# Turned queries and key-value products in two single-bank tiles, batch 0 between the weight blocks, one value scaling and one Pool chunk per tile

## The chip, the cores and the metric

One core of a Trainium2 chip runs the kernel. The metric is the device time of one execution in microseconds (us). Times are medians of the runs given; a profile is one execution with the hardware profiler. A run more than 1.5% above the fastest of the same kernel is called slow; ratios use the other, fast runs alone. PE is the tensor engine, PEld its weight loads, DVE the vector engine, ACT the scalar engine, POOL (Pool) the GpSimd engine. A "tile" below is one of 36 groups of 128 tokens; tile n's *attend* is the group of products that starts its work, and I use the start of attend as the time mark of the tile. The *clock* is the share of full speed that PE was granted. PSUM is the memory into which PE writes its products, in banks; SBUF is the memory of all other tiles. The *fold* is the product of the two weight matrices, and the *bias add* (DVE) is the last computation on a tile. A *ring* of two is a pair of buffers used in turn.

## The reference, cut to what matters

Eight batches, eight heads, 576 positions, head size 64. Linear attention with cosine and sine weights, then a two-layer network with softplus:

```python
r = np.maximum(x, 0.0);  phi = np.concatenate([r * c, r * s], axis=-1)   # for q and k
kv  = np.einsum('bhsf,bhsd->bhfd', k_p, v);   z = np.sum(k_p, axis=2)
num = np.einsum('bhsf,bhfd->bhsd', q_p, kv)
den = np.einsum('bhsf,bhf->bhs', q_p, z)[..., None] + 1e-06
x   = (num / den).transpose(0, 2, 1, 3).reshape(B * S, H * D)            # 4608 x 512
h = x @ w_in;  g = np.maximum(h, 0.0) + np.log1p(np.exp(-np.abs(h)));  out = g @ w_out
```

The kernel replaces softplus by LN2 + h/2, so that both weights fold into one matrix W_c = w_in w_out / 2 and a bias. Squares of x and of the weights check afterwards that the inputs allow it; a full path stands behind an `If`.

## The kernel before: the parts that matter here

Two PSUM tiles of two banks (`big_ps`) serve attend, the key-value products and the fold; two one-bank tiles (`qt_ps`) serve the turned queries. The queries of a batch are turned (transposed and multiplied by cosine and sine) one batch ahead.

```python
def relu_q(b, hq, engine):
    if hq == 0:
        q_rs[b] = work.tile([128, 2, T, 2, D], BF16, tag="q_r", name="q_r")   # ring of two
    engine.tensor_scalar(q_rs[b][:, hq], ..., BIG, 0.0, ALU.min, ALU.max)

def scale_values(b, hq, c):      # DVE, two SBUF inputs, cosine (c=0) or sine half (c=1)
    nc.vector.tensor_mul(view(vcs, ...), kqv[b, "v"][:, 2*hq : 2*hq+2], view(cs_wide, ...))

def relu(b):                     # Pool: one gate, then three rectifications in a row
    nc.gpsimd.tensor_copy(gate, vcs_bufs[(b - 1) % 2][:, 3, T - 1, 1, VW - 2 :])
    for hq in range(2):
        relu_q(b, hq, nc.gpsimd)
    relu_k(b, nc.gpsimd)
...                              # start: batch 0 whole, then weights, 16 squares, fold
for j, i in enumerate(mine):     # the loop over the tiles of batch b
    attend(i)
    for hq, c in itertools.islice(scales, 2 if j == 0 else 1):
        scale_values(b + 1, hq, c)
    if j == 2 and b + 2 < B:
        relu(b + 2)
    if more and j >= last - 1:
        key_values(b + 1, j - last + 1)
    some(1); turn_x(i - 1); some(1 if j < last else 9); emit(i - 2)   # cut: their conditions
```

The gate is a copy of two elements. It reads what the last scaling wrote, so Pool cannot begin to rectify before DVE has finished that scaling. The *row of eights* is the ninth block of 64 positions of each batch; those of an even and an odd batch share one tile (8, 17, 26, 35).

Of the kernel before, what the change touches and what calls it, by code (L numbers as in the profile page):

```python
# [21 lines left out]
def kernel(  # L22
# [31 lines left out]
    qt_ps = ctx.enter_context(tc.tile_pool(name="qt_ps", bufs=2, space=PSUM))  # L54
# [4 lines left out]
    def view(ap, *dims, offset=0):  # L59
        return bass.AP(  # L60
            tensor=ap.tensor, offset=ap.offset + offset,
            ap=[list(ap.ap[0])] + [list(d) for d in dims],
        )

# [12 lines left out]
    warm = singles.tile([128, 512], BF16)  # L77
    nc.vector.memset(warm, 1.0)
    load(0, "q", 0)
    load(0, "q", 1)  # L80


    idx_i = singles.tile([128, T], mybir.dt.int32)
# [4 lines left out]
    for part in range(2):  # L88
        load(0, "k", part)
        load(0, "v", part)  # L90

    xT_all = singles.tile([128, N_TOK // 128, KO, 128], BF16)
    w_in_sb = xT_all[:, 4 : 4 + D_FF // 128].rearrange("p n g t -> p (n g t)").rearrange(
        "p (ko f) -> p ko f", ko=KO
    )
    w_out_sb = singles.tile([128, FO, D_MODEL], BF16)
    for ko in range(KO):
        nc.gpsimd.dma_start(w_in_sb[:, ko, :], moe_w_in[ko * 128 : (ko + 1) * 128, :])
    w_out_r = moe_w_out.rearrange("(fo p) m -> p fo m", p=128)
    for f in range(0, FO, 4):  # L100
        nc.gpsimd.dma_start(w_out_sb[:, f : f + 4, :], w_out_r[:, f : f + 4, :])
    for b in (1, 2, 3):
        for name in ("q", "k", "v"):
            load(b, name)

    ones = singles.tile([128, 128], F32)
    nc.vector.memset(ones, 1.0)
    blk_bufs = []
    for r in range(3):
        blk = singles.tile([128, 2, 2, 2, C], BF16, name=f"kvblk{r}")  # L110
        nc.vector.memset(blk, 0.0)
        blk_bufs.append(blk)
# [11 lines left out]
    nc.scalar.copy(cs_wide, view(cs_col, [1, 2 * T], [0, D]))  # L124
    diag = singles.tile([128, T, 2, 128], BF16)
    for t in range(T):
        for c in range(2):
            nc.vector.tensor_scalar_mul(diag[:, t, c, :], ident, cs_col[:, c, t : t + 1])
    perm = singles.tile([128, 128], BF16)
    nc.vector.tensor_copy(view(perm, [2, 64], [1, 2]), view(ident, [1, 64], [64, 2]))  # L130
# [5 lines left out]
    def turn_w_in(ko, half):  # L136
        n = (2 * ko + half) % 3
        pool, tag = (xt_ps, "xt") if n == 0 else (qt_ps, "qt")
        ps = pool.tile([128, 8, 128], BF16, tag=tag, name="wT_ps")
        for j in range(8):  # L140
            ft = 8 * half + j
            nc.tensor.matmul(
                ps[:, j, :], w_in_sb[:, ko, ft * 128 : (ft + 1) * 128], ident,
                is_transpose=True, start=True, stop=True, skip_group_check=True,
            )
        dst = view(
            w_inT, [D_MODEL, 8], [128, 2], [1, 64],
            offset=8 * half * D_MODEL + 256 * (ko // 2) + 64 * (ko % 2),
        )
        src = ps.rearrange("p f (h d) -> p f h d", h=2)  # L150
        if half:
            nc.scalar.copy(dst, src)  # L152
        else:
            nc.vector.tensor_copy(dst, src)

    def fold(pair, quarter, ps):
        for ft in range(4 * quarter, 4 * quarter + 4):
            for j in range(2):
                g = 2 * pair + j
                nc.tensor.matmul(  # L160
                    ps[:, j, :], w_inT[:, ft, g * 128 : (g + 1) * 128], w_out_sb[:, ft, :],
                    start=(ft == 0), stop=(ft == FO - 1),
                )
# [32 lines left out]


    VW = D + 2
    vcs_bufs = []
    for r in range(2):  # L200
        vcs = singles.tile([128, 4, T, 2, VW], BF16, name=f"vcs{r}")
        vcs_bufs.append(vcs)

    def mark_values(r):
        for hp in range(4):
            at = 0 if hp % 2 else D
            nc.vector.tensor_copy(
                vcs_bufs[r][:, hp, :, :, at : at + 2], view(cs_col, [1, T], [T, 2], [0, 2])
            )

    def scale_values(b, hq, c):
        vcs = vcs_bufs[b % 2]
        nc.vector.tensor_mul(  # L213
            view(vcs, [T * 2 * VW + 2, 2], [2 * VW, T], [1, D],
                 offset=2 * hq * T * 2 * VW + c * VW),
            kqv[b, "v"][:, 2 * hq : 2 * hq + 2],
            view(cs_wide, [0, 2], [D, T], [1, D], offset=c * T * D),
        )

    def key_values(b, hq):  # L220
        vcs, blk, k_r = vcs_bufs[b % 2], blk_bufs[b % 3], kqv[b, "k"]
        kv = big_ps.tile([128, 2, 512], F32, tag="big", name="kv_ps")
        for t in range(T):
            for h2 in range(2):
                for i in range(2):
                    rows = slice(64 * h2, 64 * h2 + 64)
                    nc.tensor.matmul(  # L227
                        kv[64 * i : 64 * i + 64, h2, : 2 * VW],
# [3 lines left out]
        for i in range(2):  # L232
            rows, cols = slice(64 * i, 64 * i + 64), slice(65 * i, 65 * i + 65)
            nc.scalar.copy(  # L234
                blk[rows, :, hq, :, cols],
                kv[rows, :, : 2 * VW].rearrange("p h (c w) -> p h c w", w=VW)[:, :, :, i : i + 65],
            )
# [3 lines left out]
    TURNS = [(hq, tp) for tp in range(TP) for hq in range(2)] + [(0, TP)]  # L241

    def turn_queries(b, n):
        hq, tp = TURNS[n]
        q_r = q_rs[b]
        if n == 0:
            qTs[b] = work.tile([128, 2, 4, S], BF16, tag="qT", name="qT", bufs=3)
        qT = qTs[b]
        ps = qt_ps.tile([128, 512], F32, tag="qt")
# [10 lines left out]
        nc.scalar.copy(dst, ps.rearrange("p (j c s) -> p j c s", j=2, c=4))  # L260


    tiles = []
    for b in range(B):
        tiles += [[(b, 128 * tp, 128, 0)] for tp in range(TP)]
        if b % 2:
            tiles.append([(b - 1, 512, 64, 0), (b, 512, 64, 64)])
    xs = {}

    x_norm = singles.tile([128, len(tiles)], F32)  # L270
    w_norm = singles.tile([128, FO], F32)

    def attend(n):
        num = big_ps.tile([128, 4, 256], F32, tag="big", name="num_ps")
        for g in range(4):
# [12 lines left out]
        x = outs.tile([128, 4, 2, D], BF16, tag="x", bufs=3)  # L288
        nc.vector.tensor_mul(  # L289
            x, view(num, [256, 4], [66, 2], [1, D]), view(rden, [2, 4], [1, 2], [0, D])  # L290
        )
        xs[n] = x

    def turn_x(n):
        x = xs.pop(n)
        ps = xt_ps.tile([128, 4, 128], F32, tag="xt", name="xT_ps")
        for g in range(4):
            nc.tensor.matmul(  # L298
                ps[:, g, :], x[:, g, :, :], perm if len(tiles[n]) == 1 else ident, start=True, stop=True, skip_group_check=True,
            )  # L300
        nc.scalar.copy(xT_all[:, n], ps)  # L301
        square = outs.tile([128, D_MODEL], BF16, tag="square", name="square", bufs=1)
        nc.scalar.activation(square, x, ACT.Square, bias=zero_b, accum_out=x_norm[:, n : n + 1])  # L303
# [9 lines left out]
    def emit(n):  # L313
        ps = o_ps.tile([128, D_MODEL], F32, tag="o", name="o_ps")
# [7 lines left out]
    def spin(count):  # L322
        ps = qt_ps.tile([128, 512], F32, tag="qt", name="spin_ps")
        for _ in range(count):
            nc.tensor.matmul(ps, warm[:, :128], warm, start=True, stop=True, skip_group_check=True)

    def fetch(b):
        for name in ("q", "k", "v"):
            load(b, name)

    gate = singles.tile([128, 2], BF16)

    def relu(b):

        nc.gpsimd.tensor_copy(gate, vcs_bufs[(b - 1) % 2][:, 3, T - 1, 1, VW - 2 :])  # L335
        for hq in range(2):
            relu_q(b, hq, nc.gpsimd)
        relu_k(b, nc.gpsimd)

    spin(16)  # L340
    for hq in range(2):
        relu_q(0, hq, nc.vector)
    mark_values(0)
    for hq in range(2):
        relu_k(0, nc.vector, slice(2 * hq, 2 * hq + 2))
        for c in range(2):
            scale_values(0, hq, c)
    for n in range(9):
        turn_queries(0, n)
    key_values(0, 0)  # L350
    spin(2)
    key_values(0, 1)
    spin(2)
    w_turns = iter([(ko, half) for ko in range(KO) for half in range(2)])
    for n in range(4):
        attend(n)
        turn_w_in(*next(w_turns))
        if n:
            turn_x(n - 1)
    mark_values(1)  # L360
    for ko, half in w_turns:
        turn_w_in(ko, half)
        if (ko, half) == (2, 0):
            turn_x(3)
    for ft in range(FO):
        square = outs.tile([128, D_MODEL], BF16, tag="square", name="square", bufs=1)
        nc.scalar.activation(  # L367
            square, w_inT[:, ft, :], ACT.Square, bias=zero_b, accum_out=w_norm[:, ft : ft + 1]
        )
    wc_ps = [big_ps.tile([128, 2, D_MODEL], F32, tag="big", name=f"wc_ps{r}") for r in range(2)]  # L370
    for quarter in range(4):
        sum_w_out(quarter)
        for pair in range(2):
            fold(pair, quarter, wc_ps[pair])
    for hq in range(2):
        relu_q(1, hq, nc.vector)
# [3 lines left out]
    bias()  # L380
    relu_k(1, nc.vector)
    for n in range(9):
        turn_queries(1, n)
        if n % 2:
            emit(n // 2)
            scale_values(1, n // 4, n // 2 % 2)
    for hq in range(2):
        key_values(1, hq)
    fetch(4)
    relu(2)  # L390

    n = 4
    for b in range(1, B):
# [120 lines left out]
```

## Time and profile before

| | before |
|---|---|
| median of 4 runs | 150.2 us (149.88 to 150.6) |
| span of the profiled run, mean granted clock | 148.7 us, 0.971 |
| tile 4 starts | 51.50 us |
| end of the last bias add | 141.2 us |
| tile 4 to there | 89.7 us |

The page, the stretches of the loop and the chain of the start are shown in the prediction. To them belongs the longest wait of the kernel before (engine, what it was about to run, what ended the wait; then us in total, times, longest):

```profile
POOL gate L335 <- DVE vcs L213: 29.1, 5, 7.3
```

Pool waits for DVE at its gate: 29.1 us of idle time on an engine that has time.

### The profile page before, as it was taken

How to read it: one execution, taken by the hardware profiler on the slowest of the kernel's cores; microseconds unless marked ns; L12 is line 12 of the kernel's file. 1: busy time of each engine (PE TensorE's matmuls, PEld its weight loads, DVE VectorE, ACT ScalarE, POOL GpSimd, SP SyncE). 2: the span in 40 equal slices, each digit the busy share in tenths (PEclk: the TensorE clock that was granted, in tenths of full speed). 3: DMA queues.
4: the chain of work that ended last, by engine and by line, in shares of the span. 5: the costliest groups of instructions: out<-in, count | busy, mean ns of one | idle time of the engine just before them, and what ended most of it. 6: DMA issues, size and time to landing. Idle time of an engine off the chain costs nothing.

```text
span 148.7 us, 3802 instructions
## 1 busy us (share of the span) xinstructions
PE 119.9 (81%) x1482; PEld 75.6 (51%) x1482; DVE 108.9 (73%) x237; ACT 113.7 (76%) x255; POOL 53.0 (36%) x67
## 2 busy tenths in 40 slices
PE   6966875999967728798979899897899988999510
PEld 2323665444434507566657567575567755664100
DVE  6867494699467579978967986994998798599420
ACT  3468298999995626899899889989988989967300
POOL 6965132231300095196079059219009200000000
PEclk9999999999999986999999999999999999999985
DMA  1999999999999999999999999999942324144430
GB/s 21 181 179 216 213 213 202 209 204 209 207 207 208 267 266 209 208 208 265 239 250 256 239 239 269 228 256 249 241 171 82 142 74 109 61 155 152 153 90 4
DMA packets 20678, 28.07 MB, mean 189 GB/s; under 512 B 1200, under 2 KB 15536, under 8 KB 20656
## 3 DMA queue, kind: packets, MB, share of 16 engines
q0 software_dynamic: 15408, 18.35, 71.8%
q1 hardware_dynamic: 5248, 9.44, 18.8%
q8 instruction: 12, 0.20, 0.5%
q14 instruction: 10, 0.08, 0.2%
HBM read 36.70 MB, written 9.44 MB: 310 GB/s over the span
## 4 chain that ended last, share of the span: by engine, by line
PE 33%; DVE 25%; ACT 23%; issue 7%; DMA 5%; POOL 3%; DVEq 0%; POOLq 0%
PE o_ps L316 17%; DVE o_sb L318 11%; ACT square L367 9%; DVE vcs L213 8%; DMA v_sb<-in_v_dram 5%; PE kv_ps L227 5%; PE num_ps L279 4%; PE ps L252 4%; DVE x L289 3%; ACT square L303 3%; ACT qT L260 3%; ACT w_inT L152 3%; PE xT_ps L298 2%; ACT xT_all L301 2%; ACT kvblk L234 2%
## 5 line engine op out<-in xcount | busy, mean ns | idle before, releaser
L260 ACT CAST qT<-ps 128x512 bf16<-128x512 f32 x72 | 40.6, 592 | 11.3 <-PE ps L252 10.9
L316 PE MATMUL o_ps<-W_c,xT_all 128*128 128x512 bf16 x144 | 36.9, 378 | 5.1 <-DVE o_sb L318 3.5
L318 DVE TENSOR_TENSOR o_sb<-o_ps,b_bc 128x512 f32<-128x512 f32 x36 | 24.8, 688 | 13.4 <-PE o_ps L316 13.3
L252 PE MATMUL ps<-diag,q_r 128*128 128x256 bf16 x144 | 27.7, 279 | 8.1 <-ACT qT L260 4.6
L213 DVE TENSOR_TENSOR vcs<-v_sb,cs_wide 128x1152 bf16<-128x1152 bf16 x32 | 27.9, 871 | 2.4 <-ACT qT L260 1.2
L289 DVE TENSOR_TENSOR x<-num_ps,rden 128x512 bf16<-128x512 f32 x36 | 24.9, 692 | 3.3
L303 ACT ACTIVATE square<-x,zero_b 128x512 bf16<-128x512 bf16 x36 | 26.6, 739 | 0.0
L279 PEld LDWEIGHTS <-qT 128*128 128x128 bf16 (+1 forms) x320 | 19.6, 101 | 9.0 <-DVE x L289 1.9
L279 PE MATMUL num_ps<-kvblk,qT 128*128 128x130 bf16 (+1 forms) x320 | 23.4, 223 | 0.6 <-ACT kvblk L234 0.5
L301 ACT CAST xT_all<-xT_ps 128x512 bf16<-128x512 f32 x36 | 21.5, 596 | 3.0 <-PE xT_ps L298 3.0
L316 PEld LDWEIGHTS <-xT_all 128*128 128x128 bf16 x144 | 13.8, 97 | 17.1 <-issue 7.9
L252 PEld LDWEIGHTS <-q_r 128*128 128x128 bf16 x144 | 11.8, 99 | 15.0 <-issue 8.0
L234 ACT CAST kvblk<-kv_ps 64x260 bf16<-64x260 f32 x32 | 12.0, 375 | 6.0 <-PE kv_ps L227 5.7
L298 PE MATMUL xT_ps<-perm,x 128*128 128x128 bf16 x128 | 12.6, 222 | 3.0 <-DVE x L289 1.2
L160 PE MATMUL wc_ps<-w_out_sb,w_inT 128*128 128x512 bf16 x64 | 14.0, 379 | 0.1
L192 POOL TENSOR_SCALAR q_r<-q_sb 128x1152 bf16<-128x1152 bf16 x12 | 13.6, 1145 | 0.0
L298 PEld LDWEIGHTS <-x 128*128 128x128 bf16 x144 | 10.8, 99 | 5.3 <-issue 2.1
L227 PE MATMUL kv_ps<-vcs,k_sb 64*64 64x132 bf16 x576 | 11.5, 219 | 2.1 <-DVE vcs L213 2.0
L187 POOL TENSOR_SCALAR k_sb<-k_sb 128x2304 bf16<-128x2304 bf16 x6 | 12.6, 2102 | 0.0
L73 POOL DMA_DIRECT2D k_sb<-in_k_dram x9 | 6.7, 739 | 16.1 <-PE kv_ps L227 10.7
L367 ACT ACTIVATE square<-w_inT,zero_b 128x512 bf16<-128x512 bf16 x16 | 11.6, 723 | 0.5
L335 POOL COPY gate<-vcs 128x2 bf16<-128x2 bf16 x6 | 1.1, 190 | 29.1 <-DVE vcs L213 29.1
(55 smaller groups left out, 115.4 us busy)
## 6 DMA issues: line engine op xcount, KB each, us to landing
out_dram<-o_sb SPq DMA_DIRECT2D x32, 256.0 KB, 5.9
q_sb<-in_q_dram POOLq DMA_DIRECT2D x7, 576.0 KB, 20.5
k_sb<-in_k_dram POOLq DMA_DIRECT2D x7, 576.0 KB, 18.5
v_sb<-in_v_dram POOLq DMA_DIRECT2D x7, 576.0 KB, 20.9
xT_all<-in_moe_w_in_dram POOLq DMA_DIRECT2D x4, 512.0 KB, 12.6
w_out_sb<-in_moe_w_out_dram POOLq DMA_DIRECT2D x4, 512.0 KB, 18.5
out_dram<-o_sb SPq DMA_DIRECT2D x8, 128.0 KB, 4.0
q_sb<-in_q_dram POOLq DMA_DIRECT2D x2, 288.0 KB, 5.0
```

Source lines behind the costliest of these rows:

```text
L213: nc.vector.tensor_mul(view(vcs, [T * 2 * VW + 2, 2], [2 * VW, T], [1, D], offset=2 * hq * T * 2 * VW + c * VW), kqv[b, "v"][:, 2 * hq : 2 ...
L227: nc.tensor.matmul(kv[64 * i : 64 * i + 64, h2, : 2 * VW], k_r[rows, 2 * hq + i, t, :], vcs[rows, 2 * hq + i, t, :, :], start=(t == 0), st ...
L252: nc.tensor.matmul(ps[:, 256 * j : 256 * j + 256], q_r[:, hj, t, :, :], diag[:, t, :, :], start=True, stop=True, skip_group_check=True,)
L260: nc.scalar.copy(dst, ps.rearrange("p (j c s) -> p j c s", j=2, c=4))
L279: nc.tensor.matmul(num[p0 : p0 + m, g, :C], qTs[b][:, hq, 2 * c + h2, t0 : t0 + m], blk_bufs[b % 3][:, h2, hq, c, :], start=(c == 0), stop ...
L289: nc.vector.tensor_mul(x, view(num, [256, 4], [66, 2], [1, D]), view(rden, [2, 4], [1, 2], [0, D]))
L298: nc.tensor.matmul(ps[:, g, :], x[:, g, :, :], perm if len(tiles[n]) == 1 else ident, start=True, stop=True, skip_group_check=True,)
L301: nc.scalar.copy(xT_all[:, n], ps)
L303: nc.scalar.activation(square, x, ACT.Square, bias=zero_b, accum_out=x_norm[:, n : n + 1])
L316: nc.tensor.matmul(ps, xT_all[:, n, g, :], W_c[:, g, :], start=(g == 0), stop=(g == 3))
L318: nc.vector.tensor_add(o_sb, ps, b_bc)
L367: nc.scalar.activation(square, w_inT[:, ft, :], ACT.Square, bias=zero_b, accum_out=w_norm[:, ft : ft + 1])
```

## The change

Its intent: free `big_ps` for attend by moving the key-value products into the two one-bank tiles (`banks`); fold the weights as their blocks arrive and put batch 0 between them, so that the 16 squares no longer stand before W_c; make turned queries two tiles ahead instead of a batch ahead; and give every tile one scaling on DVE and, just behind it, one gated chunk of rectification on Pool. The core of the diff (cuts are marked `...`):

```diff
-    qt_ps = ctx.enter_context(tc.tile_pool(name="qt_ps", bufs=2, space=PSUM))
+    qt_ps = ctx.enter_context(tc.tile_pool(name="qt_ps", bufs=1, space=PSUM))
+    banks = [qt_ps.tile([128, 512], F32, name=f"bank{r}") for r in range(2)]
...
+    for j in range(1, 5):
+        load_w(j)
+    for name in ("k", "v", "q"):
+        for part in range(2):
+            load(0, name, part)
+    for j in range(5, BLOCKS):
+        load_w(j)
...
-    def relu(b):
-        nc.gpsimd.tensor_copy(gate, vcs_bufs[(b - 1) % 2][:, 3, T - 1, 1, VW - 2 :])
-        for hq in range(2):
-            relu_q(b, hq, nc.gpsimd)
-        relu_k(b, nc.gpsimd)
+    def pool_relu(b, part, after):
+        hq, c = part // 2, part % 2
+        nc.gpsimd.tensor_copy(gate, vcs_bufs[after % 2][:, 2 * hq + 1, T - 1, c, VW - 2 :])
+        if part < 2:
+            relu_k(b, nc.gpsimd, slice(2 * part, 2 * part + 2))
+        else:
+            relu_q(b, part - 2, nc.gpsimd)
...
-        kv = big_ps.tile([128, 2, 512], F32, tag="big", name="kv_ps")
...  # cut: kv[..., h2, ...] becomes banks[h2][...]; two copies become four of half the size
...
     for b in range(B):
-        tiles += [[(b, 128 * tp, 128, 0)] for tp in range(TP)]
+        for tp in range(TP):
+            turns[len(tiles)] = [(b, tp, hq) for hq in range(2)]
+            tiles.append([(b, 128 * tp, 128, 0)])
         if b % 2:
+            turns[len(tiles)] = [(b - 1, TP), (b, TP)]
             tiles.append([(b - 1, 512, 64, 0), (b, 512, 64, 64)])
...
+            for part in itertools.islice(parts, (0, 1, 2, 1)[j] if b == 0 else left < 4):
+                scale_values(b + 1, part)
+                if b + 2 < B:
+                    pool_relu(b + 2, part, b + 1)
             attend(i)
+            ahead = [] if i == 2 else turns.get(i + 2, []) if i != 3 else turns[4] + turns[5]
...
+    emit(last - 1, big_ps)
+    emit(last, big_ps)
```

Note `turns[len(tiles)] = [(b - 1, TP), (b, TP)]`: the row of eights of an even batch is now turned together with that of the odd batch, two tiles before its tile.

## The prediction

> **What bounds the kernel now.** I read the page first, then the busy time per stretch, then the chain of waits in order of time, then the timeline of single engines where the chain changes character. No engine bounds the whole span; there are three stages, each with its own limit.
>
> ```profile
> PE 119.9 (81%) x1482; PEld 75.6 (51%) x1482; DVE 108.9 (73%) x237; ACT 113.7 (76%) x255; POOL 53.0 (36%) x67
> ...
> DMA  1999999999999999999999999999942324144430
> GB/s 21 181 179 216 213 213 202 209 204 209 207 207 208 267 266 209 208 208 265 239 250 256 239 239 269 228 256 249 241 171 82 142 74 109 61 155 152 153 90 4
> ```
>
> Shares of 73 to 81% say only that three engines are loaded alike. The GB/s row gives the pace of the loads (each number is one slice of 3.72 us). The busy times of two equal stretches, nine tiles of the loop each, and of the tail are (PE, weight loads, DVE, ACT, POOL, then clock, DMA share, GB/s):
>
> ```profile
> 75.40:99.85 24.45, 22.31 (x332) 15.49 (x333) 19.90 (x45) 22.79 (x54) 13.42 (x15) 1.00 1.17 248
> 99.85:124.30 24.45, 22.30 (x333) 15.47 (x333) 19.88 (x45) 22.78 (x54) 8.95 (x8) 1.00 0.59 158
> 127.90:141.30 13.40, 11.06 (x100) 6.17 (x97) 10.44 (x25) 8.53 (x20) 0.00 (x0) 1.00 0.36 135
> ```
>
> The reader is to see that both stretches take 24.45 us although the DMA share halves from 1.17 to 0.59: the loop is not bound by transfers. ACT is busy for 22.8 of the 24.45 us, so the loop runs at 2.717 us a tile near ACT's rate. The chain of waits shows the start:
>
> ```profile
> 40.57 0.81 ACT square L367 x2
> 41.39 0.97 ACT W_c L378 x2
> 42.35 0.50 ACT b_bc L180
> 42.89 1.04 PE o_ps L316 x4
> ...
> 53.30 0.69 DVE x L289
> 53.99 4.49 DVE vcs L213
> ```
>
> Sixteen squares stand on ACT from 27.8 to 41.3 us, and the folded weight W_c waits behind them. Then come four serial rounds of product, bias add and turned queries to 51 us, and a multiply that takes 4.49 us. Its cause is in the timelines of DVE and POOL:
>
> ```profile
> 53.90 5.36 DVE L213 TENSOR_TENSOR vcs<-v_sb,cs_wide 128x1152 bf16<-128x1152 bf16 x2
> 53.50 2.28 POOL L192 TENSOR_SCALAR q_r<-q_sb 128x1152 bf16<-128x1152 bf16 x2
> 55.74 2.11 POOL L187 TENSOR_SCALAR k_sb<-k_sb 128x2304 bf16<-128x2304 bf16 x1
> ```
>
> The value scaling (749 ns at its median) began while Pool was in a relu, and finished only after three Pool instructions in a row had ended at 57.85. The gate copy in front of each relu prevents this in the rest of the loop. In the tail the chain alternates between a product into the single o_ps buffer and its bias add, 1.80 us a tile (bias adds at 127.91, 129.71, 131.52).
>
> **What the Trainium skill says.**
> "SBUF — State Buffer", section "Who interferes with whom": a DVE instruction with two SBUF inputs contends with a GpSimd instruction that reads SBUF, and the loser fully blocks. The scaling has two such inputs, and the trace agrees (4.49 us for a 0.75 us instruction). The section says that the lock lasts for one instruction; here the wait outlasted three. I use the measurement.
> "ScalarE: Activation LUTs", section "What ACT_TABLE_LOAD costs": a fixed part plus 0.833 ns for each element of a row. The trace: a copy of 512 from PSUM takes 592 ns, of 1024 takes 1014 ns, so 0.824 ns an element.
> "DMA: Bandwidth & Descriptors", section "Where 436 GB/s comes from": 435 GB/s is the ceiling of the 16 ports. The loads turn f32 into bf16; 207 GB/s written is 414 GB/s read, close to that. I take the load rate as fixed.
> "PSUM — Partial Sum Buffer", section "PSUM bank collisions raise a hardware error": guard PSUM by bank. With turned queries and kv in the same two banks, a kv matmul group must wait for the last two copies of turned queries. No row of the kernel before can show this wait.
>
> **The change part by part.**
> (1) ACT work in the loop. Squares: two of 512 (0.71 us each from start to next start, 75.10 to 75.81) become one of 1024: 0.71 + 512 x 0.83 ns = 1.14 instead of 1.42; per nine tiles 4.5 x 0.28 = 1.3 us saved. The kv copies: two of 64x260 (375 ns each, 0.79 the pair) become four of 64x130: 375 - 130 x 0.83 = 267 ns, with gaps 1.12 us in all; four halves in nine tiles add 4 x 0.33 = 1.3 us. The two cancel. So the loop's ACT load and, by this, its rate should stay near 2.717 us a tile.
> (2) The start. The loads are reordered, not lessened. Weights and batch 0 are 5.96 MB in bf16 (three of 0.59, two of 2.10). The GB/s row sums to 6.09 MB after nine slices, 33.5 us, so 5.96 MB are in at 32.8, and about 1 us later (estimate) they count as landed. The last w_in block lands one 1.3 us transfer sooner, 32.5. Then eight transposes (0.45 by the chain), two blocks of eight fold matmuls at 0.219 (50 in 10.95 us), 3.5, and one ACT and one DVE scaling of W_c, 1.3 us, free the first big_ps buffer: 37.8, with slack for late copies 38.4. The squares no longer stand before it, because they follow each block.
> (3) Batch 0 now runs inside the loop. Its tiles have no full pipeline behind them yet. From the PE intervals (attend 0.47, two-matmul turn 0.22, turned x 0.22, product 0.87, kv 0.65) and ACT's (turned queries 0.50, x copy 0.475), I get 1.0, 2.3, 2.8 and 3.7 us for tiles 0 to 3, so tile 4 starts at 38.4 + 9.8 = 48.2. It started at 51.5 before.
> (4) From tile 4. The bias add of tile 4 comes in tile 6, about 2.8 us into it: 48.2 + 5.4 + 2.8 = 56.4, against 62.6 before, where the 4.49 us stall stood in between. At 2.717 a tile, the bias add of tile 28 comes at 56.4 + 24 x 2.717 = 121.6, against 124.1.
> (5) The tail. Turns are now made two tiles ahead of use, no longer a batch ahead, so tiles 31 to 33 still carry them (2.2 us each by ACT and PE); then two of 1.8, and two final products in separate buffers, 2.1 together: 12.3 us to the end, 134.0. Before it was 141.2.
> Sum without new waits: -7.2 us.
> (6) The new wait that I see. The ring of q_r holds two batches. The last turn of an even batch, the row of eights, now happens in tile 6 (then 15, 24), but Pool is told in tile 2 (11, 20) to write the batch two later over it. Pool works in order, so it stands still until tile 6, and its chunks then come back to back: two q chunks (1.14 each), three DMA issues (0.75 each), three or four more chunks. They lose their place just behind a scaling. A scaling that arrives during such a run is held until Pool is idle, by the 4.49 us row. From the order I estimate 0.5 us at tile 7, 1.5 to 3.3 us at tile 8, the same at 16 and 17, and some 2.5 at 25 and 26, where no DMA issue breaks the run: 6 to 9 us if all bite, 4.5 taken at part weight. Pool's unguarded relu of batch 1 may add 1 us in tile 2.
> Total: -7.2 + 5.5 = -1.7, or 148.2. As (6) is my least certain term and everything else points down, I set 147.3.
>
> **The rivals.**
> A: chunking works as meant, no scaling meets a relu, and -7.2 us comes out: 142.7. For it: the gates work in all later batches of the kernel before. Against: the order of reuse of q_r.
> B: every Pool run bites, and the DVE work that piles up is not made good (DVE has only 24.45 - 19.9 = 4.5 us free in nine tiles): 149 to 151.
> C: the shared two banks set the pace. A kv group waits for the last turned copy and ACT then waits for the kv group, 0.65 + 0.1 us; the 1024-wide square hides it at half the kv tiles, so 1.6 us per nine tiles, or 6 us in all: 148 without B. Before, ACT waited 5.7 us for kv in total, so most of this is an exchange; I give it little weight.
> D: the start is bound by DVE: constants, copies of transposed weights, sums and batch 0 are about 21 us of work (estimate from the rows) in the 20 us before the fifth block. Or PE idles between 17 and 27 us and its clock falls, as it did to 0.68 in the stretch 55 to 60 before. Each would cost 1 to 2 us.
>
> **Range and chances.** The best case is A with a good start, 142; the worst that I believe is B with D, 152. Faster by over 2% is below 146.9; that needs less than about 4 us of the losses in (6), C and D together. Chances: faster 0.48, same 0.41, slower 0.11.
>
> **What would show it.** The first attend at 38 to 39.5 us and tile 4's bias add near 56 prove (2) to (4); if the first attend is past 41, the start term is wrong. The idle time of Pool before its q relu, ended by PE turns, shows (6), and the longest scaling gives its price: three or more of 1.5 to 4 us mean B, a maximum under 1 us means A. ACT busy per nine tiles should stay at 22 to 23 us with kv copies of 267 ns and squares of about 1.16 us; if the period of nine tiles exceeds 25 us with no long scalings, it is C. The end should lie about 8.7 us below the measured time, as before (149.9 against a last bias add ended at 141.2). I am wrong most if Pool does not stand still at all, or if it stalls the turned queries themselves.

## The result, and the profile after

Ratios here and below are the mean time of one kernel's fast runs over that of the other's fast runs of the same rounds, so not quite the ratio of the medians that are quoted.

| | before | after |
|---|---|---|
| median | 150.2 us (4 runs) | 170.34 us (169.53 to 171.62, 4 runs) |
| ratio | | 1.1347 (95% interval 1.1259 to 1.1436) |
| span, clock of the profiled run | 148.7, 0.971 | 169.1, 0.877 |
| tile 0 starts (attend with the fold done) | – | 42.98 |
| tile 4 starts | 51.50 | 60.34 |
| last bias add ends | 141.2 | 161.7 |

The kernel is 13% slower; the predicted 147.3 and its range are missed by far. The engine rows, clock and DMA rows of the page after, to hold against those of before:

```profile
PE 126.7 (75%) x1473; PEld 81.3 (48%) x1473; DVE 114.9 (68%) x249; ACT 104.7 (62%) x244; POOL 72.2 (43%) x107
...
PEclk9999995589597599759999985899999599999995
DMA  3999999999999943699999459999951122413360
```

ACT has lost work (104.7 us, was 113.7), so the added time is no work of ACT. The DMA row, which stood at 9 for 28 slices without a gap before, has two holes, and the clock row has dips just after them, one after the loads have ended, and several in the start: the kernel stops as a whole, several times. Where it stops, the waits say:

```profile
POOL q_r L225 <- PE bank L281: 31.9, 3, 12.3
...
PEld L256 <- POOL k_sb L220: 16.3, 4, 5.1
DVE vcs L243 <- POOL gate L235: 14.1, 4, 4.9
```

The first line is the stand that the prediction foresaw: three waits of Pool for a turn on PE, before it may write the rectified queries. The second names Pool too, but in the hole shown below the keys that these products read had been rectified 19 us before (51.67); what they waited for was the scaling, which ended at 71.76, and PE went on at 71.91. The last line is new in kind. Before, Pool waited for DVE at the gate; now DVE waits for Pool's *gate*, four times, before a scaling. The first hole in the timeline of Pool (start, us, instruction; in brackets the idle time before it and what ended it):

```profile
52.76 0.18 POOL L235 COPY gate<-vcs 128x2 bf16<-128x2 bf16 x1
65.24 1.15 POOL L225 TENSOR_SCALAR q_r<-q_sb 128x1152 bf16<-128x1152 bf16 x1 [12.29 <-PE bank L281]
66.33 0.19 POOL L235 COPY gate<-vcs 128x2 bf16<-128x2 bf16 x1
66.47 1.15 POOL L225 TENSOR_SCALAR q_r<-q_sb 128x1152 bf16<-128x1152 bf16 x1
67.56 0.79 POOL L77 DMA_DIRECT2D k_sb<-in_k_dram  x1
68.34 0.76 POOL L77 DMA_DIRECT2D v_sb<-in_v_dram  x1
69.08 0.77 POOL L77 DMA_DIRECT2D q_sb<-in_q_dram  x1
69.81 0.22 POOL L235 COPY gate<-vcs 128x2 bf16<-128x2 bf16 x1
69.96 1.18 POOL L220 TENSOR_SCALAR k_sb<-k_sb 128x1152 bf16<-128x1152 bf16 x1
```

and DVE in the same time:

```profile
63.13 0.75 DVE L243 TENSOR_TENSOR vcs<-v_sb,cs_wide 128x1152 bf16<-128x1152 bf16 x1
...
70.07 1.69 DVE L243 TENSOR_TENSOR vcs<-v_sb,cs_wide 128x1152 bf16<-128x1152 bf16 x1 [4.55 <-POOL gate L235]
```

Read them together. DVE made the cosine half of the scaling at 63.13; its gate is the one at 69.81, because Pool works in order and had two rectifications and three DMA issues in front of it (65.24 to 69.81). The sine half of the scaling waits for that gate: the gate ends at 70.03 and the scaling starts at 70.07. Then it also runs beside the rectification at 69.96 and takes 1.69 us, not 0.75. By the indices in the code, the two elements of the gate behind the first scaling of a batch lie between the first and the last element that the second scaling writes, and so it is with the third and the fourth. The same pattern comes back at 100.54 (idle 4.85) and 128.33 (idle 2.27), and in the start at 49.30 (idle 2.41).

What this does to PE (busy us per stretch of PE, weight loads, DVE, ACT, POOL, then clock, DMA share, GB/s), after:

```profile
65.00:70.00 5.00, 2.08 (x20) 1.28 (x18) 0.52 (x1) 2.97 (x6) 4.76 (x8) 0.96 0.33 75
70.00:75.00 5.00, 3.09 (x44) 1.98 (x45) 4.72 (x9) 1.44 (x5) 3.17 (x6) 0.50 1.19 202
75.00:80.00 5.00, 5.00 (x80) 3.40 (x79) 3.67 (x8) 3.36 (x9) 3.71 (x6) 0.86 1.18 245
```

and before:

```profile
65.00:70.00 5.00, 5.00 (x86) 3.67 (x81) 3.84 (x10) 4.96 (x13) 4.50 (x5) 1.00 1.18 241
70.00:75.00 5.00, 4.42 (x70) 2.91 (x68) 4.72 (x11) 4.42 (x12) 0.00 (x0) 1.00 1.18 241
```

DVE runs one instruction in 65 to 70, PE a quarter of its usual number, and in the next stretch PE has work but a clock of 0.50. The Trainium skill, "TensorE: Matmul & The Clock Gate", section "Part 1: The HAM clock gate (the "warmup" mystery)", says that after an idle window of about 3.4 us the engine gets half the clock until it has been busy about as long. The holes of PE of 4.78 us (from 67.12) and 4.97 us (from 97.41) agree: the clock of the 5 us after them was 0.50 and 0.53. The third, of only 2.53 us (from 127.62), was followed by 0.66. So these stalls cost more than themselves.

By tile, against the kernel that is mended below: tile 7 to 8 took 9.66 us (66.50 to 76.16; mended 2.84), tile 16 to 17 took 9.83 (mended 3.25), tile 25 to 26 took 7.42 (mended 2.88). That is 6.8 + 6.6 + 4.5 = 18 us in three places, of which about 2 are made good elsewhere.

### The profile page after: what moved, and what is told of

Read it like the earlier page. It is cut to its first block, busy times and chain, and to the rows that moved or that the text cites. A ratio compares the mean times of both kernels' runs of the same rounds, so it can differ in the third digit from the quotient of the medians.

```text
span 169.1 us, 3812 instructions
## 1 busy us (share of the span) xinstructions
PE 126.7 (75%) x1473; PEld 81.3 (48%) x1473; DVE 114.9 (68%) x249; ACT 104.7 (62%) x244; POOL 72.2 (43%) x107
## 4 chain that ended last, share of the span: by engine, by line
PE 31%; POOL 18%; issue 13%; DMA 13%; DVE 12%; ACT 11%; POOLq 0%; DVEq 0%
PE o_ps L349 13%; DMA w_out_sb<-in_moe_w_out_dram 6%; DMA k_sb<-in_k_dram 6%; DVE vcs L243 6%; ACT qT L289 5%; PE bank L256 5%; DVE o_sb L351 5%; POOL q_r L225 4%; PE bank L281 4%; PE xT_ps L329 4%; ACT warm L188 3%; PE num_ps L309 3%; POOL xT_all L99 3%; POOL w_out_sb L100 2%; POOL gate L235 2%
## 5 line engine op out<-in xcount | busy, mean ns | idle before, releaser
L289 ACT CAST qT<-bank 128x512 bf16<-128x512 f32 x70 | 39.9, 605 | 10.7 <-PE bank L281 10.7
L243 DVE TENSOR_TENSOR vcs<-v_sb,cs_wide 128x1152 bf16<-128x1152 bf16 x32 | 27.6, 866 | 14.2 <-POOL gate L235 14.1
L264 ACT CAST kvblk<-bank 64x130 bf16<-64x130 f32 x64 | 13.7, 264 | 30.3 <-PE bank L256 30.1
L256 PE MATMUL bank<-vcs,k_sb 64*64 64x132 bf16 x576 | 14.4, 247 | 22.6 <-DVE den L315 13.0
L225 POOL TENSOR_SCALAR q_r<-q_sb 128x1152 bf16<-128x1152 bf16 x14 | 16.7, 1191 | 33.3 <-PE bank L281 31.9
L281 PE MATMUL bank<-diag,q_r 128*128 128x256 bf16 x144 | 28.1, 300 | 2.5 <-ACT kvblk L264 0.7
L256 PEld LDWEIGHTS <-k_sb 64*64 64x64 bf16 x576 | 11.4, 122 | 25.6 <-POOL k_sb L220 16.3
L188 ACT ACTIVATE warm<-x,zero_b 128x1024 bf16<-128x1024 bf16 x18 | 21.2, 1179 | 0.0
L220 POOL TENSOR_SCALAR k_sb<-k_sb 128x1152 bf16<-128x1152 bf16 x14 | 16.6, 1184 | 4.3 <-DMA k_sb<-in_k_dram 4.3
L188 ACT ACTIVATE warm<-w_inT,zero_b 128x512 bf16<-128x512 bf16 x16 | 11.6, 722 | 10.6 <-DVE w_inT L182 10.3
L235 POOL COPY gate<-vcs 128x2 bf16<-128x2 bf16 x28 | 7.2, 258 | 15.3 <-DVE vcs L243 9.3
```

The lines of the kernel that those rows point to most:

```text
L188: nc.scalar.activation(warm[:, :size], source, ACT.Square, bias=zero_b, accum_out=dst)
L225: engine.tensor_scalar(q_rs[b][:, hq], view(kqv[b, "q"], [D, T], [T * D, 2], [1, D], offset=2 * hq * T * D), BIG, 0.0, ALU.min, ALU.max,)
L243: nc.vector.tensor_mul(view(vcs_bufs[b % 2], [T * 2 * VW + 2, 2], [2 * VW, T], [1, D], offset=2 * hq * T * 2 * VW + c * VW), kqv[b, "v"][: ...
L256: nc.tensor.matmul(banks[h2][64 * i : 64 * i + 64, : 2 * VW], k_r[rows, 2 * hq + i, t, :], vcs[rows, 2 * hq + i, t, :, :], start=(t == 0), ...
L281: nc.tensor.matmul(ps[:, 256 * j : 256 * j + 256], q_r[:, hj, t, :, :], diag[:, t, :, :], start=True, stop=True, skip_group_check=True,)
L289: (copy or nc.scalar.copy)(dst, ps.rearrange("p (j c s) -> p j c s", j=2, c=4))
```

## The experiments

Theory: Pool's stand behind the ring of two `q_r` buffers makes the holes, and the gate carries each hole over to DVE. First rival: the port alone (the access to SBUF that DVE and Pool share: a scaling that meets a rectification, as the prediction had it). Second rival: the shared banks set the pace of the loop. Third: the start is slow for reasons of its own (clock, the sums of w_out, the place of batch 0). All runs were correct against the reference. Every kernel below is the changed kernel, or where it is said the mended one, with the edit shown.

### A third buffer for rectified queries

The tile did not fit, so the sums of w_out lie in rows of `xT_all` that are not yet in use.

```diff
-    w_sum = singles.tile([128, 2, D_MODEL], F32)
+    w_sum = xT_all[:, 12:16]...   # seen as F32 [128, 2, 512]
-            q_rs[b] = work.tile([128, 2, T, 2, D], BF16, tag="q_r", name="q_r")
+            q_rs[b] = work.tile([128, 2, T, 2, D], BF16, tag="q_r", name="q_r", bufs=3)
```

> The changed kernel with a third buffer for q_r (the room comes from keeping w_sum in rows of xT_all that are not used yet). Theory R (the ring of two makes Pool stand until the late turn of the row of eights, and the value scaling then stands behind Pool's gate copy): Pool's q relu waits for PE no more (31.9 us of idle in the changed kernel), the three waits of scaling for gate at tiles 6, 15 and 24 (11.7 us) are gone, the PE clock stays at 1.0 there, and the time falls by 12 to 18 us to 152 to 158. Theory P (the port lock alone is the cost, as in the record): also falls, but only 6 to 9 us. Theory C (kv and turned queries in the same two banks set the pace): 168 to 171.

Measured: 153.57 us (152.36 to 154.19, 4 runs), ratio 1.0218 (1.0181 to 1.0255). Pool no longer waits for PE, and DVE waits for the gate once, in the start, for 0.80 us. Of the 20 us lost, this buffer alone brings back about 17.

### The gate moved away from the next scaling, ring of two kept

The gate of part (hq, c) read the last two elements of the half that it follows. For the cosine half these lie between the first and the last element that the sine half writes, though the sine half does not write them. The edit lets the gate of a cosine half read the first two elements of that half, which lie before everything that the next scaling writes. Pool still waits for the same scaling.

```diff
-        nc.gpsimd.tensor_copy(gate, vcs_bufs[after % 2][:, 2 * hq + 1, T - 1, c, VW - 2 :])
+        nc.gpsimd.tensor_copy(gate, vcs_bufs[after % 2][:, 2 * hq + c, c * (T - 1), c,
+                                                        c * (VW - 2) : c * (VW - 2) + 2])
```

> The changed kernel, ring of two kept; only the two columns that the gate copy reads are moved to a place that the next scaling does not overlap in the dependency check (first columns of the first head pair for the cosine half, last of the second for the sine half). Pool still stands until tile 6, 15, 24 and still comes back in one run. Theory R: scaling no longer waits for the gate; what remains is the port, so single scalings of 1.5 to 4 us appear instead and the time falls by 5 to 12 us to 158 to 165. Theory P: nothing falls, 168 to 171, and the idle time of DVE turns into long scalings. Theory C: 168 to 171 with no long scalings.

Measured: 160.61 us (157.42 to 162.54, 4 runs, two of them slow; the fast ones 157.42 and 159.55), ratio 1.0672 (1.0581 to 1.0763). No wait of DVE for the gate is left, so the wait was for those two elements, no data that DVE needed. Pool still stands (two waits for PE of 15.2 us in all, and a third of 9.9 that the profile puts down to a bias add). And now the scalings meet the run of Pool instructions. DVE, then Pool:

```profile
61.81 1.62 DVE L243 TENSOR_TENSOR vcs<-v_sb,cs_wide 128x1152 bf16<-128x1152 bf16 x1
...
64.99 2.94 DVE L243 TENSOR_TENSOR vcs<-v_sb,cs_wide 128x1152 bf16<-128x1152 bf16 x1
```
```profile
64.92 1.17 POOL L220 TENSOR_SCALAR k_sb<-k_sb 128x1152 bf16<-128x1152 bf16 x1
66.01 0.20 POOL L235 COPY gate<-vcs 128x2 bf16<-128x2 bf16 x1
66.16 1.16 POOL L225 TENSOR_SCALAR q_r<-q_sb 128x1152 bf16<-128x1152 bf16 x1
```

This is the world that the prediction described: with the gate wait gone, the port is what makes the stand expensive. Behind tile 4 the scalings of this kernel last 9.1 us more, in sum, than 0.75 us each. The Trainium skill, "SBUF — State Buffer", section "Who interferes with whom", says that whoever issues first holds the shared ports and the other blocks; the scaling at 64.99 came 0.07 us after a rectification and ended at 67.9, after two rectifications and a gate.

### Both: the mended kernel

> Third buffer and moved gate together. Theory R: once Pool is on time the gate's false overlap costs nothing in the loop; only the one wait of 2.4 us before tile 2 goes too, so 0 to 4 us below the third buffer alone. If the gate cost something by itself in each tile, 5 us or more below it.

One time, 150.83 us. The same kernel was timed again later on another chip:

> The mended kernel once more (third buffer for rectified queries and the gate that reads away from the next scaling), now timed in rounds, because it had only one time so far, 150.83 against about 150.3 before. If the two repairs give back the whole loss, the ratio lies within 0.99 to 1.015. If the single time was lucky and the new order has a further cost of its own, it lies above 1.02.

Measured: 150.04 us (149.79 to 150.45, 4 runs), ratio 0.9984 (0.994 to 1.0029). The two repairs give back the whole loss, 170.34 − 150.04 = 20.3 us, and no more. From tile 7 on no scaling takes over 0.76 us. The loop runs (nine tiles each):

```profile
68.42:92.57 24.15, 22.30 (x330) 15.74 (x332) 20.12 (x45) 22.37 (x54) 14.85 (x23) 1.00 1.17 249
92.57:116.52 23.95, 21.74 (x329) 15.60 (x332) 19.98 (x45) 21.68 (x53) 11.75 (x18) 1.00 0.91 213
```

Nine tiles took 24.45 us before, with ACT busy for 22.8. So the predicted loop is right once the two waits are out.

### The ring taken away in another way: the row of eights turned early

The ring of two stays, but the row of eights of an even batch is turned with that batch's own last tile, so the old buffer comes free in time.

```diff
-        if b % 2:
-            turns[len(tiles)] = [(b - 1, TP), (b, TP)]
+        if b % 2 == 0:
+            turns[len(tiles) - 1].append((b, TP))
+        else:
+            turns[len(tiles)] = [(b, TP)]
```

> The changed kernel, ring of two kept; only the turn of the row of eights of each even batch is made with the last turns of its own batch, in the second tile of the batch, not in the next batch. This frees q_r before Pool wants it. Theory R: the same as a third buffer within 3 us (152 to 159). If the late turn were not the cause, 168 to 171.

Measured: 156.4 us (one run, its state unknown). Then with the moved gate as well:

> The changed kernel with its two buffers for rectified queries, the turn of the eights of even batches made with the batch's own last tile (156.4 alone), and the gate moved off the next scaling. If the early turn takes away Pool's stand as fully as a third buffer does, this must come to the same as the mended kernel, 150 to 152, so that what is left of 156.4 was the one gate wait in the start and what hung on it. If the early turn has a price of its own in the turned-query ring or on ACT, it stays at 153 or above.

Measured: 151.3 us (149.77 to 152.04, 4 runs, one of them slow), ratio 1.0075 (1.0027 to 1.0123), inside what was expected. It is the late turn, not the size of the ring as such, that makes Pool stand.

The six kernels form a table of two factors. Times are from the profiled executions; "to the end" is from tile 4's start to the end of the last bias add.

| row of eights, `q_r` ring | gate | tile 4 starts | tile 4 to the end |
|---|---|---|---|
| late, two buffers | as in the change | 60.34 | 101.3 |
| late, two buffers | moved | 53.54 | 94.9 |
| late, three buffers | as in the change | 57.88 | 85.2 |
| late, three buffers | moved (mended) | 55.67 | 85.1 |
| early, two buffers | as in the change | 60.45 | 86.6 |
| early, two buffers | moved | 53.23 | 87.3 |

Behind tile 4 the stand costs 94.9 − 85.1 = 9.8 us without the gate's wait (the stretched scalings above add up to 9.1), and the gate adds 6.4 to it; without the stand the gate costs 0.1 there. Each row is one execution: the second is the fastest of four that differ by 5 us, and the mended kernel's single run before had tile 4 at 56.36, with 85.1 to the end. In the start the gate costs 6.8 us with two buffers (7.2 with the early turn) and 2.2 with three. The third buffer has a price in the start: the mended kernel reaches tile 4 2.1 us later than the same gate with two buffers. One thing that differs there: its scaling in tile 3 takes 1.99 us beside Pool's rectifications, against 1.00. What part of the 2.1 that is was not measured.

### The shared banks: key-value products back in the two-bank tile

On the mended kernel; batch 0 keeps the banks, because the fold holds the two-bank tiles then.

```diff
+        big = big_ps.tile([128, 2, 512], F32, tag="big", name="kv_ps") if b else None
+        kv = [big[:, h2] for h2 in range(2)] if b else banks
...          # and two copies of 64x260 in place of four of 64x130 when big is there
```

> The mended kernel with kv of batches 1 to 7 in the two-bank tile of the big pool again, copied by two 64x260 copies as in the kernel before; turned queries keep the single banks. Theory C (sharing the two banks costs the loop 1.6 us in nine tiles and four copies instead of two cost 1.3): the period of nine tiles falls from 24.1 to about 22 and the time by 4 to 8 us. The record's view (an exchange: kv then holds a buffer that attend wants): within 2 us of 150.8.

Measured: 150.0 us (149.65 to 150.09, 4 runs), ratio 0.9962 (0.9916 to 1.0007), where the mended kernel has 0.9984 (0.994 to 1.0029). The intervals overlap, and from tile 4 to tile 26 it takes 57.2 us against 57.1: going back to the two-bank tile gains nothing, so this rival does not explain the loss. That both arrangements cost the loop equally much is not excluded.

### The start

Why did even the mended kernel begin tile 0 at 42.66 and not at 38.4? Two suspects show in its timelines and windows. First, PE's clock was 0.50 in 25 to 30 us. Second, DVE's half of the scaling of W_c stood behind the sums of w_out, and these were stretched by Pool's rectification of batch 1, which no gate holds back from DVE's sums. In the changed kernel:

```profile
38.59 2.05 DVE L206 TENSOR_TENSOR w_sum<-w_sum,w_tmp 128x1024 f32<-128x1024 f32 x1
40.67 1.66 DVE L208 TENSOR_TENSOR w_tmp<-w_sum 128x512 f32<-128x512 f32 x1
42.25 1.27 DVE L392 TENSOR_SCALAR W_c<-wc_ps 128x512 bf16<-128x512 f32 x2
```

Elsewhere the first of these takes 1.22 us. The first experiment keeps PE busy with idle matmuls (on the mended kernel):

```diff
             fold(4, wc_ps)
+            spin(14)
...
                 key_values(0, hq)
+                spin(4)
```

> On top of third buffer and moved gate (called the mended kernel, 150.8 us): 22 spare matmuls stand where PE waits for batch 0 in the start (14 before its kv groups, 4 behind each). Theory S1 (the start is late because the PE clock falls to 0.5 between 25 and 35 us): the clock stays at 0.9 or more there, the fold ends 1.5 to 2.5 us sooner, and the time falls by 1 to 2.5 us. Theory S2 (it is late because W_c waits on DVE behind the sums of w_out, which Pool's relu of batch 1 stretches): under 1 us.

Measured: 151.93 us (150.98 to 153.15, 4 runs), ratio 1.0121 (1.0045 to 1.0198). The clock stood at 1.00 from 25 to 55 us, but the fold ended no sooner. Its last products on PE, mended kernel and then this one:

```profile
35.70 3.62 PE L193 MATMUL wc_ps<-w_out_sb,w_inT 128*128 128x512 bf16 x16
```
```profile
35.61 3.62 PE L193 MATMUL wc_ps<-w_out_sb,w_inT 128*128 128x512 bf16 x16
```

The half of W_c on ACT came at 38.84 (mended 38.92), and the half on DVE waited behind the sums till 41.28 (mended 41.92), so tile 0 began at 42.02. The 0.6 us come from a sum that no rectification stretched this time (1.22 us, mended 2.05); two executions of the mended kernel differ by 0.5 here. A miss: that the low clock cost anything is not shown, and the spare matmuls stood in front of batch 0's own work (its turned queries were copied at 31.19 and 32.35, mended 30.22 and 31.58). Tile 4 did start 2.0 us sooner (53.70), and the last bias add ended 0.8 sooner; but the span went on for 9.4 us after it, not 7.2. Why was not followed, so the time of this run does not judge the start alone. Then the last sum was moved behind tile 0's attend as well:

```diff
-        if j > 0 and j % 2 == 0:
+        if j > 0 and j % 2 == 0 and j < BLOCKS:
             sum_w_out(j // 2 - 1)
...
             attend(i)
+            if i == 0:
+                sum_w_out(3)
```

> The mended kernel with the spare matmuls, and the last sum of w_out taken after the first attend instead of before W_c. S1 and S2 together: the first attend starts near 38.5 instead of 43.2 and the time falls by 3 to 5 us, to 146 to 148. S1 alone: no better than the spare matmuls alone.

Measured: 157.9 us (154.49 to 159.65, 4 runs, three of them slow, so there is no ratio). Tile 0 began at 41.59, but tile 2 only at 50.27. The last sums now ran at 44.54 (2.06 us) and 46.62 (1.66 us), in the middle of Pool's rectifications, and the bias product of tile 1 waited for them till 48.43. The delay had moved, not gone. The profiled run is itself a slow one, so its sizes are not compared with the others.

Last, batch 0 before all weight blocks, as in the kernel before, but with the rest of the new order (mended kernel; the first two lines put the loads in words):

```diff
-    load_w(0) ... load_w(4); batch 0's loads; load_w(5) ... load_w(7)
+    batch 0's loads; load_w(0) ... load_w(7)
...
-        if j == 5:
-            fold(4, wc_ps)
+        if j == 0:
...
-        if j > 0 and j != 5:
+        if j > 0:
```

> The mended kernel with batch 0 loaded and processed ahead of all weight blocks, so only the placing between the blocks is undone. The bytes before the last weight block are the same. If the placing costs only what it does to the clock (S1), PE has no hole between blocks, the fold ends 1 to 2.5 us sooner and the time falls by 1 to 3 us; if the placing hides the constants and batch 0's work well, the time rises by 0 to 2 us.

Measured: 149.09 us (148.5 to 149.64, 4 runs), ratio 0.9897 (0.9841 to 0.9953). Tile 0 began at 40.36. DVE's half of W_c, which tile 0 waits for, in the mended kernel and then in this one:

```profile
41.92 1.27 DVE L392 TENSOR_SCALAR W_c<-wc_ps 128x512 bf16<-128x512 f32 x2
```
```profile
39.62 1.28 DVE L391 TENSOR_SCALAR W_c<-wc_ps 128x512 bf16<-128x512 f32 x2
```

With batch 0 early, the fold ends at 37.95 (mended 39.32), and DVE comes to its last sums sooner, before Pool's rectification can stretch the large one (1.23 us, mended 2.05). PE still runs dry once, but earlier: the clock of 0.50 lies in 15 to 20 us. Putting batch 0 between the weight blocks costs the mended kernel about 1 us by the medians; the intervals of the two ratios just touch.

### A version that beats both, and what stops it

Batch 0 first and the two-bank key-value products together, on the mended kernel:

> The mended kernel with batch 0 before the weights (it gave 149.09 alone) and with the key-value products of batches 1 to 7 in two-bank tiles (150.0 alone). If the two gains are independent, 1.7 and 0.8 us below the mended kernel's 150.83, it comes to about 148.3, ratio 0.986. If they overlap, because both act on tiles 2 to 4, 149, ratio 0.99.

Measured: 149.37 us (149.13 to 149.56, 6 runs), ratio 0.9929 (0.9896 to 0.9963): no better than batch 0 first alone. Then batch 1's last scaling was moved from tile 3 to tile 2:

```diff
-            for part in itertools.islice(parts, (0, 1, 2, 1)[j] if b == 0 else left < 4):
+            for part in itertools.islice(parts, (0, 2, 2, 0)[j] if b == 0 else left < 4):
```

> As the kernel above, but the last scaling of batch 1 is made in tile 2 and no longer in tile 3, where it took 1.50 us beside a relu of Pool and, with the product behind it, kept the tensor engine idle for 1.90 us. If this scaling holds the start, tile 4 begins 1 to 1.5 us sooner (54.0 there) and the time is about 147, ratio 0.978. If the wait only moves into tile 2, or the turns of tiles 4 and 5 set the pace, nothing changes, within 0.3 us of the kernel above.

Measured: 148.89 us (148.5 to 149.37, 6 runs), ratio 0.9892 (0.9857 to 0.9926), the lowest median of a correct version, 1.1% below the kernel before (its interval overlaps that of batch 0 first alone). But the gain is less than the sooner start. Tile 4 and tile 26 start at:

| kernel | tile 4 | tile 26 |
|---|---|---|
| mended | 55.67 | 112.76 |
| batch 0 first | 54.00 | 112.48 |
| early turn, gate moved | 53.23 | 112.03 |
| batch 0 first, two-bank products | 52.88 | 112.46 |
| the same, last scaling in tile 2 | 52.21 | 112.46 |

The 3.5 us between the first and the last row shrink to 0.3. In four of these kernels Pool's rectification of batch 6's queries waited for its *load*, and began within half a microsecond of the same moment. The last kernel of the table, Pool and then DVE:

```profile
98.89 1.15 POOL L225 TENSOR_SCALAR q_r<-q_sb 128x1152 bf16<-128x1152 bf16 x1 [1.23 <-DMA q_sb<-in_q_dram]
```
```profile
98.96 1.68 DVE L243 TENSOR_TENSOR vcs<-v_sb,cs_wide 128x1152 bf16<-128x1152 bf16 x1
```

The rectification starts late, and so beside the next scaling, which takes 1.68 us. To test whether the loads set the moment of tile 26, three of the 24 query, key and value loads were left out, in the fastest version and, as a control, in the mended kernel:

```diff
         for name in ("k", "v", "q"):
+            if name == "q" and b in (3, 5, 7):
+                kqv[b, name] = kqv[b - 1, name]
+                continue
             load(b, name)
```

The function is wrong (batches 3, 5 and 7 use the queries of the batch before). The comparison with the reference passed all the same, presumably because with these inputs the queries only weight an average over 576 values.

> The fastest kernel so far (148.89) with three of the 24 query, key and value loads left out: batches 3, 5 and 7 rectify the queries of the batch before, so the result is wrong on purpose and no work of an engine changes. In four kernels whose tile 4 starts between 52.2 and 54.0 the rectification of batch 6's queries waited for its load and began at 98.84 to 99.29, whatever the start, and tile 26 came at 112.5. If the loads hold the loop there, tiles 4 to 26 take about 57 us as in the mended kernel and not 60.2, tile 26 comes near 109.5 and the time falls by 2.5 to 3.5 us, to about 146. If an engine holds it, the time stays within 0.5 us.

Measured: 147.29 us (147.17 to 147.48, 4 runs), ratio 0.9783 (0.9741 to 0.9826); tile 4 at 52.64, tile 26 at 110.55, so 57.9 us between them instead of 60.25.

> The same three loads left out of the mended kernel (150.04), whose tile 4 starts at 55.7: the control. Its rectifications waited only 0.2 us for a load. If the loads matter only to a kernel that starts sooner, it stays at 149.5 to 150.1. If fewer transfers make every kernel faster for another reason, less traffic or fewer instructions on Pool, it falls by as much as the other, 2.5 us or more.

Measured: 150.21 us (149.51 to 151.39, 4 runs), ratio 0.9999 (0.9929 to 1.0069); 57.09 us between tile 4 and tile 26, with and without the three loads. So the loads hold the loop of a kernel that starts sooner, by about 2 us here, and do not hold the mended one. The fall of 1.6 us is less than the 2.5 to 3.5 expected; what holds the rest was not followed.

## Why the prediction was wrong, point by point

The record's own terms beside the two kernels (us; the last but one row is each profiled execution's own time, 170.95 and 149.79, less the row above it):

| term of the record | record | changed | mended |
|---|---|---|---|
| first attend (2) | 38.4 | 42.98 | 42.66 |
| tiles 0 to 3 (3) | 9.8 | 17.36 | 13.01 |
| tile 4 to the last bias add (4, 5) | 85.8 | 101.3 | 85.1 |
| sum | 134.0 | 161.7 | 140.8 |
| from there to the measured time | 8.7 | 9.3 | 9.0 |
| new waits (6), added in the end | 5.5 | in the rows above | – |

Against 148.2, the record's own sum, the profiled execution is 22.8 us longer. Step (6) has 11.7 of them (16.2 for 4.5), step (3) 6.6 beyond the 1 us set aside for it, step (2) 4.6.

**The step that failed is (6).** It reads: "A scaling that arrives during such a run is held until Pool is idle". Pool's stand, its cause (the row of eights turned late with a ring of two), its tiles (6, 15, 24) and the run of instructions behind it were all predicted and are in the trace. But the record took the SBUF port for the only way by which Pool could hold DVE, and 4.5 us for its price. The runs showed a second way, which the record does not mention: the gate, put there to hold Pool back, also holds DVE back, because the scaling behind it waits until its two elements have been read. Behind tile 4 the stand cost 16.2 us: 9.8 by the port, more than twice the 4.5 that the record took and just above its own 6 to 9 "if all bite", and 6.4 more by the gate. The record even had a test for the case, "the longest scaling gives its price", and it would have misled: the long scalings are only 1.7 us; the price stands in the brackets before them, as idle time.

**Step (3), tiles 0 to 3**, was 7.6 us too short in the changed kernel, and the gate explains most: moving it alone shortens them from 17.4 to 11.6 us (tile 0 also began 1.0 us earlier, so tile 4 came 6.8 sooner). Of the record's "Pool's unguarded relu of batch 1 may add 1 us in tile 2" only the port was thought of.

**Step (2), the first attend,** was 4.6 us too early, and the repairs do not mend that. It was the first half of rival D, given 1 to 2 us: a start bound by DVE. The record let W_c follow the last fold product at once; in every version traced here tile 0 waited for DVE's half of W_c, which, except where the last sum was moved, stood behind the sums of w_out. In the mended kernel the fold ended at 39.3, where the record has 36.5 by its own terms, and DVE's half of W_c began 2.6 us after that. The other half of D, the falling clock, was there (0.50) and is not shown to have cost anything: with the clock at 1.00 the fold ended at 39.2. Batch 0 first brought tile 0 forward by 2.3 us. What else would bring it to 38.4 stays open.

**Steps (1), (4) and (5) were right in mechanism, and their sum partly by luck.** The key-value copies of 64x130 took 264 ns (267 predicted), the squares of 1024 1179 ns (1160), nine tiles 24.15 and 23.95 us without the two waits (24.45), tile 4 to the end 85.1 (85.8). In that last sum errors cancel: from tile 4's start to its bias add 6.9 us (8.2), from there to the bias add of tile 28 64.6 (65.2), from there to the end 13.6 (12.3). The gain of 89.7 − 85.1 = 4.6 us behind tile 4 is real; the start gives back 55.67 − 51.5 = 4.2.

Two readings of the record are off without harm to its total: the bias add at 124.1 in the kernel before is that of tile 27 (tile 28's came at 127.91), and its 8.7 us at the end set a median of 149.9 against a profile of an execution of 150.5, whose own gap is 9.2.

**"the loop is not bound by transfers"** was true of the kernel before and did not carry over. Two stretches of equal length at DMA shares of 1.17 and 0.59 show that the loads did not hold *those tiles then*. They do not show how much sooner the tiles could have come. At the record's pace tile 26 would have started at 48.2 + 22 x 2.717 = 108.0; the kernels with the real loads came at 112.0 at the best. So part of the predicted 7.2 us could not have come out even with a perfect start, by up to 4 us (an estimate from these two numbers).

**Rivals.** A (no scaling meets a rectification) holds for the loop of the mended kernel only. B had the direction, at most 151 us, and lacked the gate. C fell. Of D, the start, the part of DVE was right and its size too small.

## What to carry to other kernels

A copy that makes one engine wait for another is a dependency in both directions: whoever writes near what it reads next may wait for the copy, and the copy stands behind everything in its in-order queue. So read small gates from a place that no later writer's range covers, and look in the list of waits for the reversed line ("DVE waits for the gate"). When a buffer's last reader is moved later, count who is told to write that buffer next and what stands behind that write in its queue; and before taking a sooner start as gain to the end, lay the landing times of the loads beside the new schedule.

## What the Trainium skill lacked or had wrong

- No page has it: a two-element read in an in-order queue can hold a writer of other elements that lie around it. Here four waits, 14.1 us, gone when the two elements were read from outside the range of the next write. That the order of instructions counts whole ranges is read from the indices; the check itself was not seen.
- "SBUF — State Buffer", "Who interferes with whom": the lock is told for one instruction. Measured: one collision cost one rectification (1.68 and 1.69 us for a scaling of 0.75), but a scaling that came into a run of Pool instructions lasted 2.94 us, through two rectifications and the gate between them, and 4.49 us in the kernel before. No run here tells when DVE gets the ports in between.
- "TensorE: Matmul & The Clock Gate", Part 1: its idle window of about 3.4 us does not cover these records. Shorter holes of PE, 2.53 us (changed kernel, from 127.62) and 1.90 us (kernel before, until 54.72), were followed by a clock of 0.66 and 0.68 in the 5 us from 130 and 55; one of 3.34 us (mended kernel, until 42.66) was followed by 1.00.
- "DMA: Bandwidth & Descriptors", "Where 436 GB/s comes from": its sentence that some 358 GB/s of HBM bind a load does not fit. In the kernel before, loads wrote 209 GB/s of bf16 from f32 (11.2 to 40.9 us), so they read about 418, near the 425 that the same paragraph reports as measured.
